# Attention and a routed MoE on one Trainium2 core: loads of q, k, v held to three in flight, and the stores of x moved

## The chip, the cores and the metric

The kernel runs on one core of one Trainium2 chip. The metric is the device time of one execution in microseconds (us). The core has a matrix engine (TensorE, "PE" in the profile; "PEld" is its weight load, which overlaps it), a vector engine (VectorE, "DVE"), a scalar engine (ScalarE, "ACT"), GpSimd ("POOL") and SyncE ("SP"), which here does nothing but issue DMAs and wait for them. Sixteen DMA engines move data between HBM and the on-chip memory. Matmul results land in PSUM, everything else on the chip is in SBUF.

## The reference, cut to what matters

```python
# q, k, v: (8 batches, 8 heads, 576 rows, 64), f32
kv  = einsum('bhsd,bhse->bhde', k, v)            # one 64x64 state for a head
out = einsum('bhsd,bhde->bhse', q, kv)
x   = out / sqrt(mean(out**2, -1) + 1e-6) * g_norm
x   = x.transpose(0, 2, 1, 3).reshape(4608, 512)  # N rows, D = 512
# MoE with early exit: E = 8 experts, F = 1024
do  = (x @ w_skip) > 0
e   = argmax(x[do] @ w_gate, 1);  gate = its softmax weight
y   = gate * (relu(x[do] @ w1[e]) @ w2[e])        # each row by its one expert
out = x;  out[do] = x[do] + y
```

## The kernel before, in words

**Order.** The whole program is written out by hand in one manual schedule: what stands first in the code is issued first on its engine. Two planning tables matter. `at(step, part, job)` puts a job at a place of a step, and a loop over `NU = 36` steps calls the places in the order `early`, `values`, `mid`, `norm`, `pe`, `end`. `portions` says in which steps the state of which batch is summed.

**Attention.** A step works on a unit: half of the heads of 256 rows of one batch. Two units make a pair (`nq`), and there are 18 pairs: two for each batch, and after every four batches one pair of the ninth rows that are left over. In a step PE turns q of the next unit (`turn`, L460, copied to SBUF by ACT as `qT`), multiplies q with the state and with the folded gate columns in one go (`values`, L498, and L508 for the left-over pairs), and sums a portion of k-times-v for the next batch (`state`, L383, eight matmul records for each group of 64 rows). ACT squares (L514) and takes roots (L529), DVE sums squares (L522) and scales (`xl`, L545), POOL multiplies by g (`xb`, L615). When all 18 groups of a batch are summed, ACT copies the state to `both` (L390), POOL and DVE each copy it twice into the block matrix `kvd` (L395 and L394), PE turns it (L400) and multiplies it with the gate weights (`state_m`, L408), and ACT copies those results into `kvd` (L412). All of these small products share one PSUM tile, `g_ps`.

**Loads.** SP issues every load of q, k, v (96 of them, 288 KB each) and most stores of x (`out_dram<-xb`, 256 KB each) in one order. Buffers: three of k and v, two of q, six of xb. A load of k and v is issued when the batch three before it has been summed. The framework gives DMAs eight semaphores in turn, so that a DMA waits for the one eight before it. A pair's x is stored in two halves when POOL has made it; of some pairs POOL issues the first half itself (L649).

**Gating.** Three groups of row tiles (`ends = [12, 22, 36]`) are gated while attention runs: `choose` on DVE, `rank` (running counts, matmuls into `g_ps`, L696 to L702), `number` on DVE (`oha_k`, L728). After the second group the experts are sorted by their counts (`rank_experts`, whose result `order_i` SP reads before it loads the first expert's w1, L337), and the first 192 rows of expert 0 are found among the batches 0 to 4 (`early`: 22 small matmuls L926, a sum on DVE L930, a small matmul L936) and gathered by POOL (L919). Batches 0 to 4 are the pairs 0 to 10. That gather waits for the stores of those pairs.

**Experts.** From about 117 us on the eight experts run one after the other (lines from L1157 on), nearly all of it PE. Their weights stand in two sets of buffers, `wpool_a` and `wpool_b`. The tile w2 of `wpool_a` is called `room` during attention, because until the first expert's w2 is loaded (L347) it only holds some small inputs. The gathers of later rows (L1148) wait for all stores of x.

Of the kernel before, what the change touches and what calls it, by code (L numbers as in the profile page):

```python
# [17 lines left out]
def kernel(  # L18
# [47 lines left out]
    P = 128  # L66
# [3 lines left out]
    NF = B // 4  # L70
    FQ = 4 * NQ + 1
    NT = NF * FQ * 2
    E, F = moe_w1.shape[0], moe_w1.shape[2]
    G = E + 1
    KD = D + G
# [34 lines left out]
    g_ps = ps_g.tile([P, 512], FP32)  # L110
    GB = 4 * KD + 8 * G

    kts, vts, qts = {}, {}, {}

    def load_part(t, src, b, j):

        js = slice(j, j + 1)
        nc.sync.dma_start(
            out=t[:, js, :, :].rearrange("p j c d -> p j (c d)"),
            in_=src[b].rearrange("(j a) (p c) d -> (a p) j (c d)", a=2, c=C)[:, js, :])  # L120

    def load(pool, tag, src, b):
        t = pool.tile([P, 4, C, D], FP32, tag=tag, name=tag)
# [120 lines left out]
    nc.vector.tensor_copy(out=eorder[:, :], in_=eorder_i[:, :])  # L244
    ebase = keep.tile([P, E], FP32)
    nc.vector.tensor_copy(out=ebase[:, :], in_=ebase_i[:, :])
    exp_f = keep.tile([P, E], FP32)
    nc.vector.tensor_copy(out=exp_f[:, :], in_=exp_i[:, :])
    col_f = keep.tile([P, CK], FP32)
# [101 lines left out]
            tc.add_manual_dep(ins.ins, behind.ins.name, WAIT, reason="gathers first")  # L351


    kvTs, boths = {}, {}

    def own(b, w):

# [17 lines left out]
    def state(b, some):  # L375

        kt, vt = kts[b], vts[b]
        for i in some:
            u, c = divmod(i, C)
            for w in range(2):  # L380
                for a in range(2):
                    r = slice(a * 64, (a + 1) * 64)
                    nc.tensor.matmul(  # L383
                        out=sum_ps[w * 64:(w + 1) * 64, a, u, :],
                        lhsT=kt[r, 2 * u + w, c, :], rhs=vt[r, 2 * u + w, c, :],
                        start=(c == 0), stop=(c == C - 1), skip_group_check=True)
        if some.stop < 2 * C:
            return
        both = att_pool.tile([P, 2, 2 * D], FP32, tag="both", name="both", bufs=1)
        nc.scalar.copy(out=both[:, :, :].rearrange("p u (a d) -> p a u d", a=2), in_=sum_ps)  # L390
        boths[b] = both
        cols = slice(G, G + 2 * D)
        for w in range(2):
            nc.vector.tensor_copy(out=other(b, w)[:, :, cols], in_=both[w * 64:(w + 1) * 64, :, :])  # L394
            nc.gpsimd.tensor_copy(out=own(b, w)[:, :, cols], in_=both[w * 64:(w + 1) * 64, :, :])  # L395

    def state_t(b):
        both = boths.pop(b)
# [38 lines left out]

    late = []
    todo = {}
    WAIT = mybir.DependencyInfo(mybir.DependencyClass.Sync, mybir.DependencyReason.SCHED_ONLY)  # L440

    def at(step, part, job):
        todo.setdefault((step, part), []).append(job)
# [323 lines left out]
    order_i = keep.tile([1, E], I32)  # L767
    is_at = keep.tile([P, E, E], FP32)

    def count_tokens(name, pool):  # L770
# [3 lines left out]

    def rank_experts():

        key = count_tokens("key", gat_pool)
        nc.vector.scalar_tensor_tensor(out=key[:, :], in0=key[:, :], scalar=float(E),
                                       in1=eorder[:, :], op0=ALU.mult, op1=ALU.add)
# [16 lines left out]
        order_f = gat_pool.tile([P, E], FP32, tag="order_f", name="order_f")  # L796
        yield
        nc.vector.tensor_reduce(out=order_f[:, :], in_=gt[:, :, :], axis=AX.X, op=ALU.add)
        yield
        nc.vector.tensor_copy(out=order_i[:, :], in_=order_f[0:1, :])  # L800
        yield
        nc.vector.scalar_tensor_tensor(
            out=colid_i[:, :].rearrange("p (r c) -> p r c", c=CK),
            in0=order_f[:, :].unsqueeze(2).to_broadcast([P, E, CK]), scalar=float(RSPACE // 128),
            in1=col_f[:, :].unsqueeze(1).to_broadcast([P, E, CK]), op0=ALU.mult, op1=ALU.add)
# [92 lines left out]
    def early():  # L898
# [24 lines left out]
        def put():  # L923
            scale(now[0])
            for t in range(NE):
                nc.tensor.matmul(out=ps, lhsT=oha_k[:, t, :],  # L926
                                 rhs=bv[:, t, :, :].rearrange("p c i -> p (c i)"), start=(t == 0),
                                 stop=(t == NE - 1), skip_group_check=True)
            rows = gat_pool.tile([P, 2], FP32, tag="rows1", name="rows1")
            nc.vector.tensor_reduce(out=rows[:, :], in_=ps.rearrange("p (c i) -> p c i", i=2),  # L930
                                    axis=AX.X, op=ALU.add)
            gather(rows[:, 0:1], P, 0)

            def put_more():
                more = g_ps[:, GB + 4:GB + 5]
                nc.tensor.matmul(out=more, lhsT=again[0, 64][:, :], rhs=rows[:, 1:2], start=True,  # L936
                                 stop=True, skip_group_check=True)
# [28 lines left out]
    for b, n in starts.items():  # L966
        if b:
# [6 lines left out]
                step += 1  # L974
            assert i == 2 * C and step < n and step - len(counts) > over - 1
            at(step, "early", lambda b=b: state_t(b))
            at(step, "pe", lambda b=b: state_m(b))
            over = step
        at(over, "end", lambda b=b: load_kv(b + 3, range(4 if b > 1 else 2)))
# [5 lines left out]
    def gating(g):  # L985

        yield from choose(g)
        yield lambda: rank(g)
        numbers = number(g)
        yield next(numbers)  # L990
        if g == LAST - 1:
# [3 lines left out]
        if g == LAST - 1:  # L995
            yield from early()

    streams = []
    now = [0]
    at(NU - 4, "pe", lambda: load_second(0, valued[-1]))  # L1000
    for r in range(1, E):
# [10 lines left out]
    PACE = (2, 4)  # L1012
    for n in range(NU + 2):
        now[0] = n
        if 1 <= n < NU - 1:
            turn(n + 1)
        if 1 <= n <= NU:
            root(n - 1)
# [3 lines left out]
        jobs(n, "mid")  # L1022
        if THIRD + 2 <= n < NU:
            squares(n)
        done = norm(n - 1) if 1 <= n <= NU else None
        if n < THIRD + 2:
            squares(n)
# [604 lines left out]
```

## Time and profile before

| what | value |
|---|---|
| median of three runs | 369.45 us (369.28 to 370.48) |
| the profiled execution | 369.93 us, of which the span of instructions is 368.1 us |
| PE busy | 349.5 us, 95% of the span |
| DVE, ACT, POOL busy | 249.2, 144.7, 126.6 us |
| DMA | 81.70 MB, mean 222 GB/s |
| granted TensorE clock | 1.00 |

The page divides the span into 40 slices of 9.2 us and gives each engine's busy share of a slice in tenths. "Idle before, releaser" is the time in which an engine stood still before an instruction, and what ended it; "issue" there means that the profile shows nothing that the engine waited for. Instructions are themselves fetched by DMA: those transfers are the queues of the kind "instruction".

### The profile page before, as it was taken

The page shows a single profiled execution, that of the slowest core. Times are in us where ns is not written, and L with a number is a line of the kernel's source. Part 1 is how long each engine was busy: PE and PEld are TensorE (multiplying, and loading weights), DVE is VectorE, ACT ScalarE, POOL GpSimd, SP SyncE. Part 2 cuts the span into 40 slices and gives each one's busy share as a digit, 9 for nine tenths or more (in the row PEclk, how much of TensorE's full clock was granted, in tenths as well). Part 3 has the DMA queues.
Part 4 walks back from the last instruction along what each step waited for, and adds up shares of the span by engine and source line. Part 5 has one row for each costly group of instructions (what it writes and reads, how often), then busy time and mean ns, then how long its engine had stood idle before and what let it go on. Part 6 is the DMA issues. An engine that isn't in the chain of part 4 may idle for free.

```text
span 368.1 us, 9568 instructions
## 1 busy us (share of the span) xinstructions
PE 349.5 (95%) x3754; PEld 304.4 (83%) x3754; DVE 249.2 (68%) x637; ACT 144.7 (39%) x418; POOL 126.6 (34%) x205
## 2 busy tenths in 40 slices
PE   8979997899889998999999999999999999999994
PEld 4768886788779668599879988988998988989983
DVE  2636677689889661776938675776776876878831
ACT  2537675466666242434204501421431430431420
POOL 8037777667776072223031203303203202002003
PEclk9999999999999999999999999999999999999999
DMA  8999999999977459972617345564663672601001
GB/s 274 383 389 387 393 389 396 401 357 328 325 247 268 116 183 367 363 250 78 230 54 251 98 198 184 176 232 123 223 231 80 241 249 56 244 1 49 11 1 54
DMA packets 32808, 81.70 MB, mean 222 GB/s; under 512 B 3242, under 2 KB 3250, under 8 KB 32756
## 3 DMA queue, kind: packets, MB, share of 16 engines
q1 hardware_dynamic: 28944, 69.48, 53.3%
q0 software_dynamic: 3792, 11.53, 9.3%
q8 instruction: 31, 0.51, 0.5%
q14 instruction: 21, 0.17, 0.1%
q10 hardware_dynamic: 20, 0.02, 0.0%
HBM read 66.80 MB, written 14.48 MB: 221 GB/s over the span
## 4 chain that ended last, share of the span: by engine, by line
PE 78%; issue 8%; DMA 5%; DVE 4%; POOL 3%; ACT 2%; SPq 0%; POOLq 0%; DVEq 0%; ACTq 0%
PE bank L1256 45%; PE bank L1188 8%; PE o_ps L498 6%; DMA v<-in_v_dram 4%; PE sum_ps L383 4%; PE bank L1176 3%; PE q_ps L460 3%; PE bank L1157 2%; DVE xl L545 1%; POOL xb L615 1%; PE g_ps L861 1%; DMA xg<-out_dram,asrc 1%; PE o_ps L508 1%; PE q_ps L861 1%; PE g_ps L762 1%
## 5 line engine op out<-in xcount | busy, mean ns | idle before, releaser
L1266 ACT COPY p<-bank 128x128 f32<-128x128 f32 (+6 forms) x70 | 20.8, 297 | 95.7 <-PE bank L1256 94.1
L1256 PE MATMUL bank<-xt,w 128*128 128x128 f32 (+5 forms) x336 | 55.5, 288 | 0.0
L1387 POOL DMA_INDIRECT out_dram<-xg,rows x14 | 14.0, 997 | 113.4 <-DVE xg L1384 111.1
L1256 PEld LDWEIGHTS bank<-xt,w 128*128 128x128 f32 x336 | 47.0, 190 | 1.9 <-DVE bank L1260 1.4
L615 POOL TENSOR_TENSOR xb<-xl,g_b 128x512 f32<-128x512 f32 x34 | 41.4, 1217 | 19.1 <-DVE rs L536 17.3
L1260 DVE TENSOR_TENSOR bank<-bank,p 128x128 f32<-128x128 f32 (+6 forms) x70 | 23.6, 337 | 29.1 <-PE bank L1256 27.7
L1256 PE MATMUL bank<-xs,s 128*128 128x128 f32 (+5 forms) x224 | 36.7, 288 | 0.0
L498 PE MATMUL o_ps<-kvd,qT 128*128 128x146 f32 x240 | 35.2, 288 | 1.3 <-DVE xl L545 1.0
L498 PEld LDWEIGHTS o_ps<-kvd,qT 128*128 128x128 f32 x240 | 31.4, 189 | 2.1 <-DVE xl L545 1.8
L1256 PEld LDWEIGHTS bank<-xs,s 128*128 128x128 f32 x224 | 31.1, 190 | 1.0 <-issue 0.5
L1188 PE MATMUL bank<-w,ht 128*32 128x128 f32 (+2 forms) x424 | 29.9, 313 | 0.0
L383 PE MATMUL sum_ps<-v,k 64*64 64x64 f32 x1152 | 24.4, 223 | 5.5 <-issue 4.6
L383 PEld LDWEIGHTS sum_ps<-v,k 64*64 64x64 f32 x1152 | 20.0, 134 | 10.0 <-issue 6.9
L545 DVE TENSOR_TENSOR xl<-o_ps,rs 128x584 f32<-128x584 f32 x32 | 24.5, 767 | 4.3 <-PE o_ps L498 0.5
L1188 PEld LDWEIGHTS bank<-w,ht 128*32 128x32 f32 (+2 forms) x424 | 18.2, 119 | 10.6 <-issue 7.2
L1256 PE MATMUL bank<-t,ht 128*128 128x256 f32 x112 | 27.0, 384 | 0.0
L522 DVE TENSOR_REDUCE rs<-sq 128x8 f32<-128x512 f32 x36 | 24.5, 680 | 3.7 <-ACT sq L514 3.6
L1256 PE MATMUL bank<-w,ht 128*128 128x256 f32 x112 | 26.5, 380 | 0.0
L1148 POOL DMA_INDIRECT xg<-out_dram,src x14 | 14.0, 998 | 36.3 <-DMA out_dram<-xg,rows 13.2
L1256 PE MATMUL bank<-t,hs 128*128 128x256 f32 x112 | 25.3, 379 | 0.0
L514 ACT ACTIVATE sq<-o_ps 128x512 f32<-128x512 f32 x34 | 20.3, 597 | 12.5 <-PE o_ps L498 11.8
L463 ACT COPY qT<-q_ps 128x512 f32<-128x512 f32 x32 | 18.8, 586 | 13.5 <-PE q_ps L460 13.3
(216 smaller groups left out, 667.5 us busy)
## 6 DMA issues: line engine op xcount, KB each, us to landing
w<-in_moe_w_dram SPq DMA_DIRECT2D x16, 2048.0 KB, 8.9
k<-in_k_dram SPq DMA_DIRECT2D x32, 288.0 KB, 6.0
v<-in_v_dram SPq DMA_DIRECT2D x32, 288.0 KB, 6.1
q<-in_q_dram SPq DMA_DIRECT2D x32, 288.0 KB, 5.8
out_dram<-xb SPq DMA_DIRECT2D x29, 256.0 KB, 6.4
out_dram<-xb POOLq DMA_DIRECT2D x7, 256.0 KB
xg<-out_dram,src POOLq DMA_INDIRECT x16
out_dram<-xg,rows POOLq DMA_INDIRECT x16
```

The costliest lines, as they stand in the source:

```text
L383: nc.tensor.matmul(out=sum_ps[w * 64:(w + 1) * 64, a, u, :], lhsT=kt[r, 2 * u + w, c, :], rhs=vt[r, 2 * u + w, c, :], start=(c == 0), stop ...
L463: nc.scalar.copy(out=qT[:, :, :, :].rearrange("p w a t -> p (w a t)"), in_=ps[:, :, :, :, :].rearrange("p w a h t -> p (w a h t)"))
L498: mm = nc.tensor.matmul(out=ps[:, w, 0:2 * PK].rearrange("p (r k) -> p r k", r=2)[:, :, cols], lhsT=qT[:, w, a, :], rhs=kvds[b % KVD][:, w ...
L514: nc.scalar.activation(out=sq[:, :, :, :], in_=heads(ps, G, G + 2 * D), func=ACT.Square)
L522: nc.vector.tensor_reduce(out=rs[:, :, :], in_=sq[:, :, :, :].rearrange("p x y (a d) -> p x (y a) d", a=2), axis=AX.X, op=ALU.add)
L545: nc.vector.tensor_tensor(out=xl[:, :, :, :].rearrange("p x y (a k) -> p x (y a) k", a=2), in0=ps[:, :, 0:2 * PK].rearrange("p x (h k) -> ...
L615: late.append((lambda eng: eng.tensor_tensor(out=xb[:, :, 4 * u * D:(4 * u + 4) * D].rearrange("p r (w x) -> p r w x", w=2), in0=xl[:, :, ...
L1148: nc.gpsimd.indirect_dma_start(out=x_of(xg, off, m), out_offset=None, in_=cut_rows(m)[:, :], in_offset=bass.IndirectOffsetOnAxis(ap=idx[:, ...
L1188: nc.tensor.matmul(out=yps[q * m:(q + 1) * m, 0:n], lhsT=ht(f)[:, off:off + m], rhs=w_sb[r][1][:, f, q * n:(q + 1) * n], start=(f == 0), s ...
L1256: nc.tensor.matmul(out=out, lhsT=lhsT(i), rhs=rhs(i), start=start and i == 0, stop=i == k - 1, skip_group_check=True)
L1260: nc.vector.tensor_tensor(out=to, in0=x, in1=y, op=ALU.add)
L1266: nc.scalar.copy(out=t, in_=x)
```

## The change

1. Each load of q, k, v from the thirteenth on also waits until the load three before it has landed (`PACED`, `DEPTH`). Stores are not counted.
2. x of the pairs 2 to 5 is written into `room` instead of an xb buffer, and is stored from the steps 20 to 23 on, behind the loads of q of batch 6. For these and all other pairs in `store_from` both halves are issued by SP, none by POOL.
3. x of the pairs 11 and later is stored from step `NU - 4` on, which is behind the load of the first expert's w2 and behind the first gathers.
4. `rank` moves from the place `pe` to `mid`, ahead of `state_m`.
5. The two copies of a state on DVE go to ACT for the batches 5 to 7 (`state_across`).
6. Sorting the experts takes three DVE instructions less (`kbase` is made beforehand, `order_i` is summed directly as integers).
7. In `early` q of the next unit is turned on PE between the 22 matmuls and the small one, and the rows are summed at the new place `squared`, behind the sum of squares of that step. Since fewer instructions stand ahead of it, DVE makes `bv`, on which the 22 matmuls work, ahead of the step's `xl`; before, it came behind the sum of squares that follows `xl`.

```diff
-        nc.sync.dma_start(
+        ins = nc.sync.dma_start(
...
+        if len(loads) >= PACED:
+            tc.add_manual_dep(ins.ins, loads[-DEPTH].ins.name, WAIT, reason="a short queue")
+        loads.append(ins)
...
         for w in range(2):
-            nc.vector.tensor_copy(out=other(b, w)[:, :, cols], in_=both[w * 64:(w + 1) * 64, :, :])
+            if b < ACROSS:
+                nc.vector.tensor_copy(out=other(b, w)[:, :, cols], in_=both[w * 64:(w + 1) * 64, :, :])
             nc.gpsimd.tensor_copy(out=own(b, w)[:, :, cols], in_=both[w * 64:(w + 1) * 64, :, :])
+    def state_across(b, w):
+        if b >= ACROSS:
+            nc.scalar.copy(out=other(b, w)[:, :, G:G + 2 * D], in_=boths[b][w * 64:(w + 1) * 64, :, :])
...
-            xbs[nq] = xb_pool.tile([P, 2, DM], FP32, tag="xb", name="xb")
+            if nq in IN_ROOM:
+                x = room[:, IN_ROOM.index(nq) * 2 * DM:(IN_ROOM.index(nq) + 1) * 2 * DM]
+                xbs[nq] = x.rearrange("p (r d) -> p r d", r=2)
+            else:
+                xbs[nq] = xb_pool.tile([P, 2, DM], FP32, tag="xb", name="xb")
...
-    store_from = {x[0]: starts[B - 3] + 2 for x in units if x[1:3] in ((0, None), (4, 0))}
+    IN_ROOM = range(2, 6)
+    store_from = {nq: starts[B - 3] - 2 + i for i, nq in enumerate(IN_ROOM)}
+    store_from.update({nq: starts[B - 3] + 2 for nq in (4 * NQ, 4 * NQ + 1)})
+    store_from.update({nq: NU - 4 for nq in range(KNOWN_PAIRS, NT // 2)})
...
-        first = int(i == 1 and b < B - 1)
+        first = int(i == 1 and b < B - 1 and nq not in store_from)
...
-            rows = gat_pool.tile([P, 2], FP32, tag="rows1", name="rows1")
...
+            turn(now[0] + 2)
+            turned_ahead.append(now[0] + 2)
+            def put_rows():
+                rows = gat_pool.tile([P, 2], FP32, tag="rows1", name="rows1")
...
-            at(now[0], "pe", put_more)
+            at(now[0], "squared", put_rows)
...
-        yield lambda: rank(g)
+        yield "mid", lambda: rank(g)
```

On SP, from the loads of q of the last batches to the first expert's weights, this stood before (`w_1851` and `w_1853` are w1 and w2 of the first expert, `order_i` the sorted experts):

```order
L653 DMA out_dram<-xb 64x1024 x3
L118 DMA q<-in_q_dram 128x576 x8
L642 DMA out_dram<-xb 64x2x512 x2
L653 DMA out_dram<-xb 64x1024 x3
L816 TENSOR_LOAD order_i
L337 ISA
L337 DMA w_1851<-in_moe_w_dram 128x4x1024
L653 DMA out_dram<-xb 64x1024 x5
L347 ISA
L347 DMA w_1853<-in_moe_w_dram 128x8x512
L653 DMA out_dram<-xb 64x1024 x3
```

And this stands there now (`w_115` is `room`, with x of the pairs 2 to 5):

```order
L674 DMA out_dram<-xb 64x1024 x3
L121 DMA q<-in_q_dram 128x576 x4
L674 DMA out_dram<-w_115 64x1024 x8
L121 DMA q<-in_q_dram 128x576 x4
L663 DMA out_dram<-xb 64x2x512 x2
L674 DMA out_dram<-xb 64x1024 x3
L835 TENSOR_LOAD order_i
L346 ISA
L346 DMA w_1846<-in_moe_w_dram 128x4x1024
L356 ISA
L356 DMA w_1848<-in_moe_w_dram 128x8x512
L674 DMA out_dram<-xb 64x1024 x10
```

Eight stores moved between the last two batches' loads of q, and no store stands between the two weight loads any more.

On PE, at the left-over rows of the first four batches, the product of the state with the gate weights stood ahead of the first group's counts before:

```order
L508 MATMUL o_ps<-kvd_170,q_403 64x73
L408 MATMUL g_ps<-gw_b,kvT 128x36 x2
L696 MATMUL g_ps<-top,ident 128x104
L699 LDWEIGHTS ut
L699 MATMUL g_ps<-ohb,ut 128x96
```

Now it stands behind them, the counts' last matmul first in these rows:

```order
L723 LDWEIGHTS ones
L723 MATMUL g_ps<-ohb,ones 128x8
L422 MATMUL g_ps<-gw_b,kvT 128x36 x2
L473 MATMUL q_ps<-ident,q 128x2x64 x4
```

`state_m` changed places with `rank`; the same happens at the second group.

On PE, at the first gather, the small matmul that moves the last 64 rows (`again`) followed at once on the matmuls that find them (`oha_k`):

```order
L926 MATMUL g_ps<-bv_1981,oha_k 128x4
L936 MATMUL g_ps<-rows_2023,again_64_243 128x1
L460 MATMUL q_ps<-ident,q 128x2x64 x4
L479 MATMUL o_ps<-ident,q 128x128 x2
```

Now the turn of q stands between them:

```order
L945 MATMUL g_ps<-bv_1948,oha_k 128x4
L473 MATMUL q_ps<-ident,q 128x2x64 x4
L957 MATMUL g_ps<-rows_2023,again_64_245 128x1
L492 MATMUL o_ps<-ident,q 128x128 x2
```

PE has work there while DVE sums the rows that the small matmul needs.

More of the change, by code (lines that the diff above doesn't have):

```diff
@@ L72 @@
     NT = NF * FQ * 2
+    KNOWN_PAIRS = 11
     E, F = moe_w1.shape[0], moe_w1.shape[2]
@@ L111 @@
     GB = 4 * KD + 8 * G
-    kts, vts, qts = {}, {}, {}
+    kts, vts, qts, loads = {}, {}, {}, []
+    PACED, DEPTH = 12, 3
+    WAIT = mybir.DependencyInfo(mybir.DependencyClass.Sync, mybir.DependencyReason.SCHED_ONLY)
     def load_part(t, src, b, j):
         js = slice(j, j + 1)
-        nc.sync.dma_start(
+        ins = nc.sync.dma_start(
             out=t[:, js, :, :].rearrange("p j c d -> p j (c d)"),
             in_=src[b].rearrange("(j a) (p c) d -> (a p) j (c d)", a=2, c=C)[:, js, :])
+        if len(loads) >= PACED:
+            tc.add_manual_dep(ins.ins, loads[-DEPTH].ins.name, WAIT, reason="a short queue")
+        loads.append(ins)
     def load(pool, tag, src, b):
@@ L246 @@
     nc.vector.tensor_copy(out=ebase[:, :], in_=ebase_i[:, :])
+    kbase = keep.tile([P, E], FP32)
+    nc.vector.scalar_tensor_tensor(out=kbase[:, :], in0=ebase[:, :], scalar=-float(E),
+                                   in1=eorder[:, :], op0=ALU.mult, op1=ALU.add)
     exp_f = keep.tile([P, E], FP32)
@@ L351, in load_second @@
             tc.add_manual_dep(ins.ins, behind.ins.name, WAIT, reason="gathers first")
-    kvTs, boths = {}, {}
+    kvTs, boths, ACROSS = {}, {}, 5
     def own(b, w):
@@ L393, in state @@
         for w in range(2):
-            nc.vector.tensor_copy(out=other(b, w)[:, :, cols], in_=both[w * 64:(w + 1) * 64, :, :])
+            if b < ACROSS:
+                nc.vector.tensor_copy(out=other(b, w)[:, :, cols], in_=both[w * 64:(w + 1) * 64, :, :])
             nc.gpsimd.tensor_copy(out=own(b, w)[:, :, cols], in_=both[w * 64:(w + 1) * 64, :, :])
+    def state_across(b, w):
+        if b >= ACROSS:
+            nc.scalar.copy(out=other(b, w)[:, :, G:G + 2 * D], in_=boths[b][w * 64:(w + 1) * 64, :, :])
     def state_t(b):
-        both = boths.pop(b)
+        both = boths[b]
         for u in range(2):
@@ L439 @@
     todo = {}
-    WAIT = mybir.DependencyInfo(mybir.DependencyClass.Sync, mybir.DependencyReason.SCHED_ONLY)
     def at(step, part, job):
@@ L766 @@
     colid_i = keep.tile([P, NCOL], I32)
-    order_i = keep.tile([1, E], I32)
+    order_i = keep.tile([P, E], I32)
     is_at = keep.tile([P, E, E], FP32)
@@ L775, in rank_experts @@
     def rank_experts():
-        key = count_tokens("key", gat_pool)
-        nc.vector.scalar_tensor_tensor(out=key[:, :], in0=key[:, :], scalar=float(E),
-                                       in1=eorder[:, :], op0=ALU.mult, op1=ALU.add)
+        key = gat_pool.tile([P, E], FP32, tag="key", name="key")
+        nc.vector.scalar_tensor_tensor(out=key[:, :], in0=top[:, :], scalar=float(E),
+                                       in1=kbase[:, :], op0=ALU.mult, op1=ALU.add)
         gt = gat_pool.tile([P, E, E], FP32, tag="gt", name="gt")
@@ L795, in rank_experts @@
                                 in1=exp_f[:, :].unsqueeze(1).to_broadcast([P, E, E]), op=ALU.mult)
-        order_f = gat_pool.tile([P, E], FP32, tag="order_f", name="order_f")
         yield
-        nc.vector.tensor_reduce(out=order_f[:, :], in_=gt[:, :, :], axis=AX.X, op=ALU.add)
-        yield
-        nc.vector.tensor_copy(out=order_i[:, :], in_=order_f[0:1, :])
+        with nc.allow_low_precision(reason="whole numbers"):
+            nc.vector.tensor_reduce(out=order_i[:, :], in_=gt[:, :, :], axis=AX.X, op=ALU.add)
         yield
@@ L803, in rank_experts @@
             out=colid_i[:, :].rearrange("p (r c) -> p r c", c=CK),
-            in0=order_f[:, :].unsqueeze(2).to_broadcast([P, E, CK]), scalar=float(RSPACE // 128),
+            in0=order_i[:, :].unsqueeze(2).to_broadcast([P, E, CK]), scalar=float(RSPACE // 128),
             in1=col_f[:, :].unsqueeze(1).to_broadcast([P, E, CK]), op0=ALU.mult, op1=ALU.add)
@@ L928, in put @@
                                  stop=(t == NE - 1), skip_group_check=True)
-            rows = gat_pool.tile([P, 2], FP32, tag="rows1", name="rows1")
[L930 to L934, printed above, removed]
+            turn(now[0] + 2)
+            turned_ahead.append(now[0] + 2)
+            def put_rows():
+                rows = gat_pool.tile([P, 2], FP32, tag="rows1", name="rows1")
+                nc.vector.tensor_reduce(out=rows[:, :], in_=ps.rearrange("p (c i) -> p c i", i=2),
+                                        axis=AX.X, op=ALU.add)
+                gather(rows[:, 0:1], P, 0)
                 more = g_ps[:, GB + 4:GB + 5]
@@ L938, in put_more @@
                 gather(more, 64, P)
-            at(now[0], "pe", put_more)
+            assert now[0] == THIRD + 2
+            at(now[0], "squared", put_rows)
+        yield
+        yield
         yield "mid", put
@@ L976 @@
             at(step, "early", lambda b=b: state_t(b))
+            for w, part in enumerate(("early", "mid")):
+                at(step, part, lambda b=b, w=w: state_across(b, w))
             at(step, "pe", lambda b=b: state_m(b))
@@ L996, in gating @@
             yield from early()
-    streams = []
+    streams, turned_ahead = [], []
     now = [0]
@@ L1014 @@
         now[0] = n
-        if 1 <= n < NU - 1:
+        if 1 <= n < NU - 1 and n + 1 not in turned_ahead:
             turn(n + 1)
@@ L1024 @@
             squares(n)
+        jobs(n, "squared")
         done = norm(n - 1) if 1 <= n <= NU else None
```

## The prediction

> **What bounds the kernel now.** I read the slices first, then the idle time of PE, then what stands on the DMA queues where PE idles. First the page's slices (40 of 9.2 us) and the stretches of 5 us that matter:
>
> ```profile
> PE   8979997899889998999999999999999999999994
> DMA  8999999999977459972617345564663672601001
> 5.00:10.00 5.00, 4.96 (x92) 2.95 (x91) 1.27 (x18) 0.72 (x3) 3.20 (x6) 1.00 1.01 367
> 20.00:25.00 5.00, 2.58 (x83) 2.22 (x81) 1.56 (x3) 1.38 (x3) 1.19 (x1) 1.00 1.05 389
> 60.00:65.00 5.00, 2.75 (x66) 2.33 (x66) 3.16 (x9) 2.65 (x8) 2.91 (x5) 1.00 1.05 399
> 95.00:100.00 5.00, 3.97 (x33) 3.73 (x34) 4.78 (x15) 3.56 (x11) 3.77 (x8) 1.00 0.98 319
> 115.00:120.00 5.00, 5.00 (x63) 4.93 (x63) 4.77 (x13) 3.34 (x14) 2.26 (x2) 1.00 0.49 192
> ```
>
> The columns of the stretches are PE, PEld, DVE, ACT and POOL busy, then clock, DMA share and GB/s. PE is full except in places of attention, and DMA is full for the first 90 us. From 110 us on PE is full again, so what attention saves before that arrives at the end, and nothing else can be saved by this change. The idle places are in the timeline of PE:
>
> ```profile
> 18.33 1.26 PE L383 MATMUL sum_ps<-v,k 64*64 64x64 f32 x68 [0.77 <-DMA v<-in_v_dram]
> 24.45 0.62 PE L383 MATMUL sum_ps<-v,k 64*64 64x64 f32 x25 [2.42 <-issue]
> 35.38 0.66 PE L460 MATMUL q_ps<-ident,q 128*128 128x128 f32 x4
> 45.85 0.66 PE L460 MATMUL q_ps<-ident,q 128*128 128x128 f32 x4
> 61.49 0.47 PE L696 MATMUL g_ps<-top,ident 128*128 128x104 f32 x2 [0.96 <-ACT kvd L412]
> 65.13 0.57 PE L383 MATMUL sum_ps<-v,k 64*64 64x64 f32 x21 [1.42 <-issue]
> 71.52 0.56 PE L383 MATMUL sum_ps<-v,k 64*64 64x64 f32 x18 [0.74 <-issue]
> 86.05 0.46 PE L696 MATMUL g_ps<-top,ident 128*128 128x88 f32 x2 [0.44 <-ACT kvd L412]
> 98.24 1.26 PE L498 MATMUL o_ps<-kvd,qT 128*128 128x146 f32 x8 [1.03 <-DVE xl L545]
> 101.80 0.69 PE L926 MATMUL g_ps<-bv,oha_k 128*128 128x4 bf16 x22 [0.65 <-DVE bv L906]
> 102.74 0.38 PE L936 MATMUL g_ps<-rows,again 128*128 128x1 f32 x2 [0.25 <-DVE rows L930]
> ```
>
> Three waits (2.42, 1.42, 0.74 us) end on "issue" in the middle of a run of equal matmuls, and a wait for a load would name it, as the one at 18.33 does. In the stretch of each there is one packet of an instruction queue among the loads; here 21.5 to 24.5 us (packets, MB, share of 16 engines), and ahead of it two lines of the whole page:
>
> ```profile
> PE 349.5 (95%) x3754; PEld 304.4 (83%) x3754; DVE 249.2 (68%) x637; ACT 144.7 (39%) x418; POOL 126.6 (34%) x205
> q8 instruction: 31, 0.51, 0.5%
> ...
> q1 hardware_dynamic: 558, 1.14, 102.9%
> q8 instruction: 1, 0.02, 2.2%
> ```
>
> The page counts 31 such packets, 0.51 MB, so 16 KB each, for 7508 matmul and weight records, so one packet is some 240 instructions, and the sums of k and v, with 68 matmuls and as many weights in 1.26 us, use one up in some 2.3 us. I read these three waits as PE out of instructions, the fetch being late behind loads. How deep the loads stand shows the timeline of SP and the median of landings:
>
> ```profile
> 18.76 0.33 SPq L118 DMA_DIRECT2D k<-in_k_dram  x1
> 19.51 0.33 SPq L118 DMA_DIRECT2D v<-in_v_dram  x1
> 20.26 0.33 SPq L118 DMA_DIRECT2D k<-in_k_dram  x1
> k<-in_k_dram SPq DMA_DIRECT2D x32, 288.0 KB, 6.0
> ```
>
> One load every 0.75 us, landing after 6.0 us: eight in flight, the engines saturated.
>
> **The change part by part.** All terms are against the profiled execution (span 368.1, time 369.93 us) and are carried over to the median of 369.45, which is 0.48 us lower.
>
> *Period of a load.* With three in flight a load cannot come faster than the 0.75 us of the rows above. The other end is a queue that runs empty between loads:
>
> ```profile
> DMA  0000000000000995966798599308796995900000
> out_dram<-xb SPq DMA_DIRECT2D x2, 256.0 KB, 3.0
> ```
>
> This is 118.8 to 122.5 us in 40 slices of 0.0925 us: two stores into an idle queue, first data 13 slices after the start, landing after 3.0 us. With 288 KB instead of 256 that is 3.1 us, over three 1.03 us a load. I take 0.80: the stretch from 5 to 10 us, when the queue was still filling, moved 367 GB/s, and 288 KB at that rate take 0.80 us. It is the nearest row, since two other loads (1.5 us of transfer) stand ahead while a third starts up for about 1.2 us. [...]
>
> *What the loads permit.* In SP's order the 16th load is the one that PE waits for at 18.33, the 38th is the second of q of batch 2 (needed at 35.38), the 50th that of batch 3 (needed at 45.85), with two stores of x between. That 16th load took 8 us because eight loads shared the engines:
>
> ```profile
> 9.97 8.02 DMA v<-in_v_dram
> ```
>
> With fewer ahead and none behind I put it at 17.0 instead of 18.0. Then the 38th lands at 17.0 + 22 x 0.80 = 34.6 and the 50th at 17.0 + 34 x 0.80 + 1.3 (two stores of 0.65) = 45.5. So of the waits before that, 0.77 and 2.42, which both go, only 0.35 us (45.85 less 45.5) is kept; q is late next. Behind this the loads gain on PE again, since k and v of a batch are not asked for before a buffer is free.
>
> *Fetches.* The waits at 65.13 and 71.52 go: -1.42 - 0.74 = -2.16. A fetch then stands behind at most three loads. If nothing changes for it, this is 0; more than the whole wait it cannot be.
>
> *Counts ahead of the gate product.* PE waited 0.96 and 0.44 us for ACT's copies out of `g_ps`. With `rank` first, PE needs only the older copy kvT. -1.40. What is queued behind the counts, L408 and ACT's L412 copies, comes about 1 us later; the matmul that reads them comes some steps later.
>
> *First gather.* `bv` made ahead removes the 0.65 us, but delays `xl` by its own 0.24, which is in the same DVE chain and hidden unless PE waits there; the 0.25 us at L936 is covered by the turn of q. I book -0.65 and leave the 0.25 for the delay of `xl`.
>
> *State copies to ACT.* DVE is full at 95 to 100 us (4.78 of 5):
>
> ```profile
> 95.08 0.69 DVE L394 COPY kvd<-both 64x256 f32<-64x256 f32 x2
> 96.12 1.06 DVE L728 TENSOR_TENSOR oha_k<-row_i,lo_i 128x256 bf16<-128x256 int32 x2
> 90.46 0.16 DVE L800 CAST order_i<-order_f 1x8 int32<-1x8 f32 x1
> 94.23 0.35 ACT L482 COPY q<-o_ps 64x256 f32<-64x256 f32 x1
> ```
>
> There 0.69 goes and a third `oha_k` of 0.53 moves in: -0.16 on the wait of 1.03. ACT takes six copies; the nearest row is the last, 0.35 us each, and ACT is at 3.56 of 5. The first of each pair stands ahead of Square: hidden for the batches 5 and 6 where DVE has room, +0.35 once for batch 7 (0 to 1.05 as bounds). The three DVE instructions less in sorting are like the third row, 0.16 us each, beside PE's work: 0.
>
> *Stores.* Moved out of the loads' time: 0 by itself, it is in the period of the loads. Eight stores ahead of the last q cost 5.2 us on the queue, in a stretch where q of batch 7 is needed only at 96.57 us (row below). Of the POOL DMAs four go: 0, POOL is not waited for. After the first expert's w2 (issued at 106.40) now stand 14 stores: 2.1 + 3.7 MB at the 389 GB/s of the stretch from 20 us end at about 121 us, and the gather that needs them is at 129.13:
>
> ```profile
> 96.57 0.64 PE L460 MATMUL q_ps<-ident,q 128*128 128x128 f32 x4
> 106.40 0.39 SPq L347 DMA_DIRECT2D w<-in_moe_w_dram  x1
> 129.13 1.06 POOL L1148 DMA_INDIRECT xg<-out_dram,asrc  x1 [10.16 <-DVE arows L1131]
> ```
>
> It is released by DVE. If that cover went, the stores would cost what they end after 129.
>
> Sum: -0.35 - 2.16 - 1.40 - 0.65 - 0.16 + 0.35 = -4.37, so 369.45 becomes **365.1 us** (the profiled execution 365.6).
>
> **The rivals.** *A, too short a queue, slower.* If three in flight give 1.03 us a load, the 50th load lands at 17.0 + 34 x 1.03 + 1.3 = 53.3, 7.5 us late, at the turn of q for batches 2 and 3. The later terms give 4.0 back: +3.5, 373.0 us. It decides from 0.93 us a load on, where 34 x 0.93 + 18.3 is 4.0 over 45.85. For it: 3.0 us into an idle queue. Against: with two loads ahead the queue is not idle. [...]
>
> *B, the fetch does not wait behind loads.* Then the waits on "issue" stay, loads or not, and -2.16 and -0.35 drop out: 369.45 - 1.86 = 367.6. For it: fetches go by a queue of their own, q8. Against: from 110 us on, with the DMA share at half (0.49 in 115 to 120), PE runs without such waits; but its instructions are longer there. [...]
>
> *C, PE gains and hands back.* PE comes earlier to 93 to 106 us, where DVE is full, and waits there for `xl`: the gain of 4.4 shrinks to what DVE gave up, about 0.2 + 0.65: 368.6, or nothing with ACT's copies exposed (1.05), 369.5. Against: DVE's chain starts from PE's products, so it comes earlier too.
>
> **How the numbers follow.** Chances: the forecast (362.5 to 366.8) 0.47; more than that, with every wait gone, below 362.5, 0.06; the middle of A (about 368) 0.09; A itself, above 370.6, 0.18; B 0.11; C 0.09. Within 0.3% (1.1 us, about what a measurement of this kernel can tell from no change, 368.3 to 370.6) come half of the middle of A and most of C: 0.12. Slower is A, 0.18; faster the rest, 0.70. The range leaves out the 0.06 below and the worse part of A: **362.5 to 372.0**; the forecast's own is 362.5 to 366.8.
>
> **What the profile would show.** Right: landings of k, v, q near 2.4 us, SP issuing one in 0.80 us, no wait on "issue" over 0.5 us at the sums of k and v, no wait of L696's successor for L412, PE idle in attention 4 to 5 us shorter. Wrong: PE waiting at the turns of q (L460's successor) for DMA q near 34, 46 or 87 us, DMA share below 0.8 in the first 90 us, landings at 2.8 us or more; or the waits on "issue" at the same size behind a shorter queue; or the first gather late, and PE waiting for xg near 105.

## The result, and the profile after

The changed kernel takes 406.75 us (median; 403.79 to 410.21) where the kernel before has 369.62 us: a ratio of 1.098 [1.095, 1.102]. The forecast was 365.1 us. The profiled execution has a span of 405.0 us, 36.9 us more than before. These are the page's lines of it: busy times, slices of PE, the clock and DMA (now 10.1 us each), and the shares of the chain that ended last:

```profile
PE 365.0 (90%) x3754; PEld 317.9 (78%) x3754; DVE 247.5 (61%) x630; ACT 147.6 (36%) x424; POOL 123.5 (30%) x201
...
PE   8876689796778689989999999999999999999994
...
PEclk9988798988969979999999999999999999999999
DMA  8878888788977994499734455266365455610101
...
PE 62%; DMA 28%; issue 5%; SPq 2%; ACT 1%; POOL 1%; DVE 1%; POOLq 0%; ACTq 0%; DVEq 0%
```

PE's idle time went from 368.1 - 349.5 = 18.6 us to 405.0 - 365.0 = 40.0 us, and the same 3754 matmul records take 15.5 us longer, because the granted clock fell in places (its mean is 0.95 instead of 1.00). DMA is at 7 to 8 tenths in the first 90 us, where it was full, and 28% of the last chain is DMA. The longest waits of PE (total, times, longest), and the places in its timeline:

```profile
PE q_ps L473 <- DMA q<-in_q_dram: 18.1, 12, 5.3
PE sum_ps L392 <- DMA v<-in_v_dram: 6.9, 6, 2.3
PE q_ps L869 <- DMA xg<-out_dram,src: 4.5, 1, 4.5
```

```profile
23.99 1.69 PE L392 MATMUL sum_ps<-v,k 64*64 64x64 f32 x68 [2.33 <-DMA v<-in_v_dram]
44.65 0.41 PE L473 MATMUL q_ps<-ident,q 128*128 128x128 f32 x2 [2.15 <-DMA q<-in_q_dram]
61.45 0.41 PE L473 MATMUL q_ps<-ident,q 128*128 128x128 f32 x2 [2.38 <-DMA q<-in_q_dram]
77.34 0.47 PE L717 MATMUL g_ps<-top,ident 128*128 128x104 f32 x2
80.66 0.44 PE L473 MATMUL q_ps<-ident,q 128*128 128x128 f32 x2 [1.99 <-DMA q<-in_q_dram]
95.38 0.41 PE L473 MATMUL q_ps<-ident,q 128*128 128x128 f32 x2 [2.50 <-DMA q<-in_q_dram]
114.24 1.34 PE L473 MATMUL q_ps<-ident,q 128*128 128x128 f32 x4 [5.28 <-DMA q<-in_q_dram]
130.06 0.44 PE L473 MATMUL q_ps<-ident,q 128*128 128x128 f32 x2 [0.40 <-DMA q<-in_q_dram]
133.19 0.38 PE L957 MATMUL g_ps<-rows,again 128*128 128x1 f32 x2 [0.45 <-DVE rows L953]
143.07 1.09 PE L869 MATMUL q_ps<-ident,xg 128*128 128x128 f32 x4 [4.53 <-DMA xg<-out_dram,src]
```

PE now waits for q at the turns of every batch from batch 2 on (the batches are numbered from 0). The profile shows no wait on issue at the sums any more, and the counts (L717) have no wait in front of them. But the small matmul of the first gather, at 102.74 us before, is at 133.19 us: 30.45 us later. From there to the end lie 271.8 us instead of 265.4, and the 4.53 us for the first gather and some 2.2 us of a low clock behind it account for that difference (a clock of 0.77 from 143 to 153 us, row below).

Why the loads are late shows the chain in order of time (start, us, what). It hangs on one landing after the other:

```profile
12.47 4.27 DMA v<-in_v_dram
16.76 3.35 DMA k<-in_k_dram
20.13 3.73 DMA v<-in_v_dram
23.87 4.84 DMA q<-in_q_dram
...
53.72 3.28 DMA k<-in_k_dram
57.02 5.05 DMA q<-in_q_dram
...
127.27 2.74 DMA q<-in_q_dram
136.25 6.69 DMA xg<-out_dram,src
```

Each row is a load that the third load behind it waited for, so from the row of 12.47 (the 14th load) to that of 57.02 (the 50th) lie twelve landings and 36 loads: 44.55 us, or 3.71 us a landing and **1.24 us a load**. The 50th lands at 62.07 us. The last load, issued at about 84.3 us before, is issued at 127.27. The rate is in the stretches (columns as in the prediction), with two places of low clock, and the landing in the table of DMA issues (count, size, median us):

```profile
18.00:58.00 40.00, 30.43 (x515) 27.16 (x516) 15.14 (x31) 15.71 (x42) 15.73 (x30) 0.83 0.82 251
115.00:120.00 5.00, 5.00 (x49) 4.52 (x50) 2.41 (x7) 1.81 (x4) 1.40 (x2) 0.50 0.86 271
143.00:153.00 10.00, 9.93 (x110) 9.19 (x111) 4.96 (x18) 5.49 (x20) 3.25 (x7) 0.77 1.03 394
```

```profile
k<-in_k_dram SPq DMA_DIRECT2D x32, 288.0 KB, 3.6
```

The same stretch of the kernel before moved 389 GB/s:

```profile
18.00:58.00 40.00, 36.82 (x766) 32.67 (x766) 25.76 (x54) 24.98 (x66) 26.58 (x51) 1.00 1.04 389
```

### The profile page after: what moved, and what is told of

Read it like the earlier page. It is cut to its first block, busy times and chain, and to the rows that moved or that the text cites. A ratio compares the mean times of both kernels' runs of the same rounds, so it can differ in the third digit from the quotient of the medians.

```text
span 405.0 us, 9564 instructions
## 1 busy us (share of the span) xinstructions
PE 365.0 (90%) x3754; PEld 317.9 (78%) x3754; DVE 247.5 (61%) x630; ACT 147.6 (36%) x424; POOL 123.5 (30%) x201
## 4 chain that ended last, share of the span: by engine, by line
PE 62%; DMA 28%; issue 5%; SPq 2%; ACT 1%; POOL 1%; DVE 1%; POOLq 0%; ACTq 0%; DVEq 0%
PE bank L1283 41%; DMA q<-in_q_dram 10%; DMA k<-in_k_dram 9%; PE bank L1215 9%; DMA v<-in_v_dram 7%; PE bank L1203 4%; PE bank L1184 2%; PE o_ps L511 2%; DMA xg<-out_dram,src 2%; SPq L674 1%; PE q_ps L473 1%; PE g_ps L880 1%; PE q_ps L880 1%; PE g_ps L783 1%; POOL out_dram L1437 0%
## 5 line engine op out<-in xcount | busy, mean ns | idle before, releaser
L632 POOL TENSOR_TENSOR xb<-xl,g_b 128x512 f32<-128x512 f32 x26 | 31.7, 1218 | 40.2 <-DVE rs L549 34.8
L473 PE MATMUL q_ps<-ident,q 128*128 128x128 f32 x128 | 25.6, 317 | 18.2 <-DMA q<-in_q_dram 18.1
L511 PE MATMUL o_ps<-kvd,qT 128*128 128x146 f32 x240 | 41.6, 323 | 0.3
L511 PEld LDWEIGHTS o_ps<-kvd,qT 128*128 128x128 f32 x240 | 37.9, 222 | 1.1 <-DVE xl L558 0.6
L473 PEld LDWEIGHTS q_ps<-ident,q 128*128 128x128 f32 x128 | 15.1, 156 | 22.9 <-issue 12.7
L392 PE MATMUL sum_ps<-v,k 64*64 64x64 f32 x1152 | 26.5, 234 | 6.9 <-DMA v<-in_v_dram 6.9
L392 PEld LDWEIGHTS sum_ps<-v,k 64*64 64x64 f32 x1152 | 22.1, 145 | 11.8 <-issue 6.9
L549 DVE RECIPROCAL rs<-rs 128x8 f32<-128x8 f32 x36 | 7.2, 199 | 37.3 <-ACT rs L542 37.3
L558 DVE TENSOR_TENSOR xl<-o_ps,rs 128x584 f32<-128x584 f32 x32 | 24.5, 767 | 3.9
## 6 DMA issues: line engine op xcount, KB each, us to landing
w<-in_moe_w_dram SPq DMA_DIRECT2D x16, 2048.0 KB, 10.1
```

What stands on the lines that cost most here:

```text
L392: nc.tensor.matmul(out=sum_ps[w * 64:(w + 1) * 64, a, u, :], lhsT=kt[r, 2 * u + w, c, :], rhs=vt[r, 2 * u + w, c, :], start=(c == 0), stop ...
L473: nc.tensor.transpose(out=ps[:, w, :, hf, :], in_=qts[b][:, 2 * u + w, c:c + 2, :], identity=ident[:, :])
L511: mm = nc.tensor.matmul(out=ps[:, w, 0:2 * PK].rearrange("p (r k) -> p r k", r=2)[:, :, cols], lhsT=qT[:, w, a, :], rhs=kvds[b % KVD][:, w ...
L558: nc.vector.tensor_tensor(out=xl[:, :, :, :].rearrange("p x y (a k) -> p x (y a) k", a=2), in0=ps[:, :, 0:2 * PK].rearrange("p x (h k) -> ...
L632: late.append((lambda eng: eng.tensor_tensor(out=xb[:, :, 4 * u * D:(4 * u + 4) * D].rearrange("p r (w x) -> p r w x", w=2), in0=xl[:, :, ...
```

## The experiments

The theory after this result: three loads in flight do not keep the DMA engines busy, a load then takes 1.24 us, and everything in attention waits for that. The rivals: the moved stores or other parts of the change do it; or the low clock is half of the loss; or the rate of a held queue is low whatever its size. Besides, the terms that the forecast had booked as gains were to be seen alone. Each ratio is against the kernel before on the same chip.

**One part undone, one part alone, other depths.** Four kernels: no load held (`PACED = 1000`); four in flight; six in flight; and the kernel before with nothing but the holding to three.

```diff
 # e1_no_pace            # e2_depth4 / e3_depth6
-    PACED, DEPTH = 12, 3      -    PACED, DEPTH = 12, 3
+    PACED, DEPTH = 1000, 3    +    PACED, DEPTH = 12, 4   (12, 6)
 # e4_before_depth3: the kernel before, load_part alone changed
+    PACED, DEPTH = 12, 3
...
+        if len(loads) >= PACED:
+            tc.add_manual_dep(ins.ins, loads[-DEPTH].ins.name, PACE_WAIT, reason="a short queue")
+        loads.append(ins)
```

> The changed kernel with no load held back; the eight semaphores alone bound the queue, as before. Theory 1 (the whole loss is the short queue: three in flight bring a load every 1.1 to 1.2 us instead of 0.75, PE waits for q and v, and its clock drops after the waits): 363 to 368 us, clock 1.00, PE waits for q and v under 2 us in all. Theory 2 (the stores put between the loads of q and behind the first weights cost a good part, since the largest waits, 5.28 us for q of batch 6 and 4.53 us for the first gather, stand there): over 373 us, with those two waits still there. A short queue's own gain, the waits on issue of 2.42, 1.42 and 0.74 us, should be lost again here by both.

> Four loads in flight instead of three. Theory 1: a load still lands in about 3.5 us, so one comes every 0.9 us, PE waits little, the clock drops in few places or none: 368 to 380 us. Theory 2: above 390 us, since the stores stand where they stood.

> Six in flight. Theory 1: the engines are saturated, 0.75 us a load, landing 4.5 us: 363 to 367 us. If instruction fetches wait behind loads, the waits on issue at the sums of k and v are smaller than with eight in flight (sum under 3 us against 4.6). Theory 2: above 373 us.

> The kernel before with nothing but the loads held to three in flight, stores where they were. Theory 1: 400 to 412 us, as the whole change or a little worse, since the stores of pairs 2 to 5 and 11 and later still stand among the loads. Theory 2: under 390 us.

| kernel | us | ratio |
|---|---|---|
| change without holding | 369.46 | 0.999 [0.996, 1.003] |
| six in flight | 375.45 | 1.013 [1.007, 1.019] |
| four in flight | 388.88 | 1.051 [1.046, 1.055] |
| three, on the kernel before | 405.53 | 1.098 [1.091, 1.104] |

The kernel before has 369.88 us on this chip. Holding to three, alone, costs all of it, and without it the rest of the change is worth nothing. The moved stores are not the cause. Only the last of the four lies in its first range. The run without holding lies just above its own (363 to 368), four in flight between its two ranges (368 to 380, above 390), and six in flight misses 363 to 367: at six, the deepest of them, the loads do not keep their rate either. The stretch from 18 to 58 us and the landing of k, first with four and then with six in flight:

```profile
18.00:58.00 40.00, 30.46 (x563) 27.32 (x555) 18.01 (x35) 17.51 (x47) 18.47 (x36) 0.86 0.88 284
```

```profile
k<-in_k_dram SPq DMA_DIRECT2D x32, 288.0 KB, 4.2
```

```profile
18.00:58.00 40.00, 33.78 (x670) 29.54 (x670) 22.15 (x46) 22.77 (x61) 22.41 (x43) 1.00 0.98 338
```

```profile
k<-in_k_dram SPq DMA_DIRECT2D x32, 288.0 KB, 5.1
```

With 3, 4, 6 and 8 in flight the rate is 251, 284, 338 and 389 GB/s, and the landing 3.6, 4.2, 5.1 and 6.0 us; landing over depth gives 1.20, 1.05, 0.85 and 0.75 us a load. A shorter queue shortened the landing, but less than in proportion.

**The clock.** bf16 products that nobody uses are given to PE ahead of the first turn of q of the batches 2 to 6, so that it does not stand idle there.

```diff
+    FILL = {2: 12, 3: 9, 4: 7, 5: 9, 6: 19}
     def turn(n):
         ...
+        if i == 0 and u == 0 and b in FILL:
+            dense(FILL[b], ps[:, :, :, :, :].rearrange("p w a h t -> p (w a h t)"))
```

> The kernel after, with PE given bf16 products of 128x512 into the tile that the turn of q then overwrites (12, 9, 7, 9 and 19 of them, 0.27 us each) ahead of the first turn of q of the batches 2 to 6, where PE waits for q in the profile after. Their results are used by nobody. Theory 'the loads set the time': in attention PE is never waited for by the loads (the SP queue waits for PE 0.8 us in all there), so the matmuls of the stretch that run at a clock of 0.5 to 0.9 run inside time that the loads take anyway. The clock then rises to 0.98 or more, PE busy holds the 15 us of new products, and the time falls only by what the low clock costs after the last load (143 to 153 us at 0.77, 2.3 us): 402 to 407 us. Rival 'half the loss is the clock': PE's 15.5 us of longer busy time are on the path, and the time falls to about 391 us.

402.15 us, ratio 1.092 [1.082, 1.101], which overlaps that of the change itself. The page's line of busy times; the stretch up to PE's wait for the first gather, in the change (to 138.54 us) and here (to 137.70 us); and that wait here:

```profile
PE 371.0 (93%) x3810; PEld 316.9 (79%) x3810; DVE 248.0 (62%) x630; ACT 147.6 (37%) x424; POOL 124.8 (31%) x201
```

```profile
0.00:138.54 138.54, 110.62 (x1766) 93.41 (x1766) 72.35 (x201) 65.94 (x173) 66.12 (x133) 0.89 0.82 258
0.00:137.70 137.70, 117.30 (x1822) 92.89 (x1822) 72.22 (x201) 65.97 (x173) 67.94 (x137) 0.95 0.86 265
```

```profile
PE q_ps L873 <- DMA xg<-out_dram,src: 1.9, 1, 1.9
```

In the trace the 56 new products take 12.95 us (about 0.23 us each, less than the 0.27 expected). So the old ones take 371.0 - 12.95 = 358.1 us instead of 365.0: 6.9 us of the 15.5 are won back. Of these, 6.3 lie ahead of the wait for the gather (110.62 against 117.30 - 12.95 = 104.35), and yet PE comes to that wait only 0.84 us earlier. Of the 4.8 us by which the span fell, 0.84 are these, 2.6 are the shorter wait itself and 1.3 lie behind it. So the low clock inside attention was mostly hidden behind the loads, as the first theory says, and 391 us is out by far. The test is partial: the other 8.6 us of low clock were not removed, and the two profiles are from different chips, on which the kernel before differs by 1.0 us.

**Count or bytes.** Three in flight, each load from batch 1 on twice the size.

```diff
-    def load_part(t, src, b, j):
-        js = slice(j, j + 1)
+    def load_part(t, src, b, j, w):      # w = 2 if b else 1, j in steps of w
+        js = slice(j, j + w)
```

> The kernel after, with the loads of k, v and q from batch 1 on made of two of the old ones each (576 KB instead of 288 KB), three at a time as before. Theory 'a fixed time per load': a load's landing has a part that does not grow with its bytes, and three of 288 KB do not cover it; with the double size it is paid half as often, the bytes in flight are those of six old loads, and the time is near that of six in flight, 373 to 379 us. Rival 'the wait itself is what costs' (SP's issue, the semaphore and the count of three, whatever the size): per byte it is halved too, but the loads then come late for the first turns that need half of one, 385 to 395 us. Rival 'rate': the engines give a single queue with three transfers only 260 GB/s, whatever their size: 404 to 408 us.

380.27 us, ratio 1.032 [1.025, 1.039], just above the first theory's range and below the second's. The stretch, the landing, and the longest wait of PE:

```profile
18.00:58.00 40.00, 31.41 (x581) 28.69 (x574) 18.31 (x37) 18.20 (x49) 18.63 (x37) 0.87 0.91 296
```

```profile
k<-in_k_dram SPq DMA_DIRECT2D x14, 576.0 KB, 6.0
```

```profile
42.58 1.09 PE L475 MATMUL q_ps<-ident,q 128*128 128x128 f32 x4 [4.62 <-DMA q<-in_q_dram]
```

The rate rises from 251 to 296 GB/s, so it is not a fixed property of a held queue. Twice the bytes land in 6.0 instead of 3.6 us; on a straight line through these two medians 1.2 us of a landing do not grow with the bytes (0.4 to 1.7 with the medians of q and v). It stays below the 338 GB/s of six single loads with the same bytes, so the bytes in flight are not all of it. How much the number in flight and the coarser steps each make is not settled.

**Where a short queue helps.** Do the waits on issue belong to the depth of the load queue? Only the loads 65 to 82 are held, to four.

```diff
-        if len(loads) >= PACED:
+        if len(loads) in PACED:
...
-    PACED, DEPTH = 12, 3
+    PACED, DEPTH = range(64, 82), 4
```

> The kernel after, with only the loads 65 to 82 held, to four in flight; all others are free as before. These are in flight when PE waits on issue at 65.0 and 71.5 us in the run without pacing (1.45 and 0.84 us). Theory 'the fetch of instructions waits behind the loads': both waits go below 0.4 us, the last load is issued some 3 to 4 us later and just in time, and the time is 366.5 to 368 us. Rival 'the fetch does not wait behind loads': the waits stay at 1.4 and 0.8 us, 369 to 371 us. If the loads are too late for the q of batch 6 or 7, PE waits there and the time is 370 to 373 us with the issue waits gone.

372.74 us, ratio 1.010 [1.006, 1.014]. The waits on issue at the sums in the run without holding, then the first wait of more than 0.7 us behind 60 us here, and the rate from 60 to 65 us:

```profile
24.08 0.69 PE L392 MATMUL sum_ps<-v,k 64*64 64x64 f32 x25 [1.88 <-issue]
...
64.98 0.57 PE L392 MATMUL sum_ps<-v,k 64*64 64x64 f32 x21 [1.45 <-issue]
71.46 0.56 PE L392 MATMUL sum_ps<-v,k 64*64 64x64 f32 x19 [0.84 <-issue]
```

```profile
73.28 0.41 PE L473 MATMUL q_ps<-ident,q 128*128 128x128 f32 x2 [1.55 <-DMA q<-in_q_dram]
```

```profile
60.00:65.00 5.00, 4.35 (x100) 3.84 (x98) 3.74 (x11) 3.32 (x10) 3.46 (x6) 1.00 0.82 282
```

Both waits on issue are gone, before PE waits for q (in their stretch it waits only 0.65 us, for `xl`), so they do belong to the depth of the load queue. Waits for q stand in their place (4.2 us in all), and the kernel is slower. It is the third of the expected cases.

That these waits are late fetches can be counted in the traces. Take PE's instructions (weight loads, matmuls and semaphore instructions) in order of start. In the kernel before, the waits of 2.42, 1.42 and 0.74 us stand behind 705, 2241 and 2497 of them: 6 x 256 and 256 apart. Every such wait at the sums, in the kernel before and in all the experiments, stands at one of these counts, or at one further whole multiples of 256 away. And those three ended 1.48, 1.49 and 1.39 us after the end of a 16 KB packet of the instruction queue. I read this as PE out of instructions, with 256 of them in a packet, close to the 240 that the prediction estimated. At the wait of 1.42 us the packet started to move when PE had 2155 instructions behind it, 86 short of the 2241.

**A milder hold, and the rest alone.** Six in flight for the loads 65 to 82; the same for the loads 21 to 34 as well; and the kernel before with the counts, `bv` and sorting items of the change, without and with that window.

```diff
 # f1_window6: the change, and
+    PACED, DEPTH = range(64, 82), 6
 # f2_two_windows6: the change, and
+    PACED, DEPTH = [*range(20, 34), *range(64, 82)], 6
 # e8_counts_bv: items 4, 6 and 7 of the change on the kernel before
+    PACED, DEPTH = 1000, 3
 # f3_counts_window6: the same, and
+    PACED, DEPTH = range(64, 82), 6
```

> The kernel before, with the counts ahead of the gate product, bv made ahead of the first gather and the three instructions less in sorting, and nothing else of the change: loads free, x stored as before, the state copies on DVE. By the prediction's terms -1.40 and -0.65 the time is 367 to 368.3 us where the kernel before has 369.5 to 369.9. Rival 'PE gains and hands back at DVE': 369 to 370 us, with a longer wait for xl near 97 us. If it is well below the run of the change without pacing (369.46), then the moved stores or ACT's copies cost what these gain.

> The kernel after, with only the loads 65 to 82 held, now to six in flight instead of four; all others free. The step from four to six takes 18 x 0.1 us = 2 us off the last load. Theory 'the fetch waits behind the loads, and six are few enough': PE has no wait on issue over 0.5 us at the sums near 65 and 71 us, q comes 1 us late at most, 367 to 369 us. Rival 'what a short queue gives to the fetch it takes from the loads': the issue waits go and waits for q of the same 1.5 to 2.5 us stand in their place, 369 to 371 us. Rival 'the fetch needs four': the issue waits stay above 0.7 us, 369 to 370 us.

> The kernel after, with the loads 21 to 34 and 65 to 82 held to six in flight; all others free. The first stretch is in flight when PE waits on issue at 24.08 us (1.88 us without pacing). Theory 'the fetch waits behind the loads': that wait falls to about 1 us, as it did with all loads at six, the loads of q of batch 2 come 14 x 0.1 = 1.4 us later, and the time is 366 to 369 us. Rival 'given back at q': PE waits for q near 36 us for 0.8 us or more, 369 to 372 us.

> The kernel before, with the counts ahead of the gate product, bv ahead of the first gather and the three instructions less in sorting, and the loads 65 to 82 held to six in flight; x stored as before, state copies on DVE. If the moved stores make the room that a short queue needs, this is slower than the same window with the moved stores, by 1 to 2 us: 369 to 371 us, with the waits for q in the place of the waits on issue. If the room is not from the stores, the two are equal within 0.5 us.

| kernel | us | before | ratio |
|---|---|---|---|
| counts, bv, sorting alone | 368.61 | 368.62 | 1.001 [0.998, 1.004] |
| change, one window of six | 366.89 | 367.00 | 1.002 [0.999, 1.004] |
| change, two windows of six | 367.41 | 367.00 | 1.001 [0.999, 1.003] |
| counts etc., one window of six | 368.19 | 367.00 | 1.004 [1.002, 1.007] |

None beats the kernel before. (The ratios are not the quotients of the two medians shown.) The times in the last three expectations were taken from chips on which the kernel before needs 369 to 370 us; here it needs 367.00, so that 366.89, just below the first range, is no gain, nor is the 367.41 with two windows, which lies in its first range. With two windows the first wait on issue falls to 0.78 us, and q takes it back 13 us later:

```profile
22.53 0.62 PE L392 MATMUL sum_ps<-v,k 64*64 64x64 f32 x25 [0.78 <-issue]
...
35.98 0.41 PE L473 MATMUL q_ps<-ident,q 128*128 128x128 f32 x2 [1.94 <-DMA q<-in_q_dram]
```

With one window of six the wait near 65 us stays at 0.90 us on the change, and at 2.28 us on the other base:

```profile
64.32 0.57 PE L392 MATMUL sum_ps<-v,k 64*64 64x64 f32 x21 [0.90 <-issue]
```

```profile
64.42 0.57 PE L392 MATMUL sum_ps<-v,k 64*64 64x64 f32 x21 [2.28 <-issue]
```

So six in flight do not remove these waits for certain. With three loads of double size, the same bytes in flight, two of them were left too (0.63 and 1.32 us). Whether the moved stores make room is not settled: the means of these two kernels lie 1.4 us apart (plus or minus 1.1), but they differ in ACT's copies of the state as well. With the counts and `bv` alone, the waits that these items were to remove are gone, and others have grown:

```profile
83.21 0.20 PE L717 MATMUL g_ps<-ohb,ut 128*128 128x80 bf16 x1 [0.57 <-DVE ohb L703]
...
96.82 1.26 PE L511 MATMUL o_ps<-kvd,qT 128*128 128x146 f32 x8 [1.19 <-DVE xl L558]
101.78 0.38 PE L954 MATMUL g_ps<-rows,again 128*128 128x1 f32 x2 [1.02 <-DVE rows L950]
```

Of the 1.40 + 0.65 us, 0.57 + 0.16 + 0.77 us come back at DVE (1.19 was 1.03, and 1.02 was 0.25). The 0.55 us left is below what the measurement tells.

## Why the prediction was wrong, point by point

*Period of a load: the step that failed.* 0.80 us was taken and 1.24 us measured, outside even the upper end of 1.03. The argument was that two loads ahead carry the engines over the start of a third. They do not: the DMA share fell from 1.04 to 0.82, and the same share moved less, too (251 / 0.82 = 306 GB/s for a full share, 389 / 1.04 = 374 before). The 0.80 was taken from the stretch of 5 to 10 us, where up to eight loads are in flight: a queue that fills, and not a short one. The 3.0 us of two stores in an idle queue, the nearer row, was put aside, and it was too low as well: with three loads in flight a landing took 3.71 us.

*What the loads permit.* The 50th load was to land at 45.5 us and landed at 62.07. The sentence that failed beside it is that the loads gain on PE again afterwards. With 1.24 us they lose at every batch, as the waits for q up to 130 us show, and the last load is 43 us late where the queue had a few us in hand. So rival A was the right case, priced at 373.0 because it let the delay end after batch 3. Reckoned its way, even 1.24 us a load gives only 380 us (17.0 + 34 x 1.24 + 1.3 = 60.5, 14.6 us late, less 4.0); the rest of the loss is the delay of the later batches, the late first gather and the low clock behind it. The middle of A among the chances (about 368 us) stands on a period between 0.80 and 1.03 us that no run shows for three in flight: it was 1.24 us there, and landing over depth gave 1.05 and 0.85 us with four and six.

*Fetches.* Right in mechanism: the waits on issue go when fewer loads are in flight (none with three and four; 1.05 us once with all loads at six, but 0.90 and 2.28 us in windows of six) and stay with eight (1.88, 1.45 and 0.84 us). With three, PE waits for v or q ahead of the first two places, which gives the fetch time as well; the window of four is the cleaner proof. Rival B falls. But the term was booked as a net gain, while the short queue that brings it delays the loads by as much or more: the single windows show the exchange.

*Counts, first gather.* The waits of 0.96, 0.44 and 0.65 us went, as said. The claim that the turn of q covers the wait for `rows` failed: 0.25 us became 0.80 us without holding and 1.02 us with these items alone. The handing back at DVE was rival C, and for these terms it was right.

*State copies.* The wait of 1.03 us for `xl` near 97 us is 0.45 us in the run without holding, more than the 0.16 us booked; 0.52 us for `xl` at 110.56 us came in its place:

```profile
97.15 1.26 PE L511 MATMUL o_ps<-kvd,qT 128*128 128x146 f32 x8 [0.45 <-DVE xl L558]
102.11 0.38 PE L957 MATMUL g_ps<-rows,again 128*128 128x1 f32 x2 [0.80 <-DVE rows L953]
...
110.56 0.74 PE L521 MATMUL o_ps<-kvd,q 64*64 64x73 f32 x32 [0.52 <-DVE xl L558]
```

*Stores.* Nothing by themselves, as booked. Named among the signs of being wrong, but given no price, was the first gather behind late loads: in the kernel before the first expert's w1 (2 MB) was issued at 91.76 us, 11.7 us ahead of the gather, and now at 133.23, 3.0 us ahead of it. The gather took 6.69 us to land, and PE waited 4.53. With four in flight w1 was issued 7.1 us ahead, the gather landed after 3.4 us, and PE did not wait. The gather was also issued 3.06 us behind the small matmul, where it was 0.68 us before; what held it is not shown.

*The clock.* The prediction did not speak of it, since it was 1.00 throughout. It is real (15.5 us of PE); of the 6.3 us that the new products won back ahead of the gather, some 5.4 were not on the path.

## What to carry to other kernels

Before a queue of transfers is shortened, take its period from landings at that depth: here a landing shrank less than the depth did, and the saturated queue's period (0.75 us) said nothing about the short one's (1.24 us). A wait that a shorter queue removes is a gain only where the loads are needed later than they land; ask at each later use how many us they are ahead. And where the loads set the pace, a stall's second cost, a lower clock, can be mostly hidden behind the next stall, as it was here (some 5.4 of the 6.3 us won back).

## What the runs showed of the hardware

The granted clock fell after some waits and not after other, longer ones. Without holding, a wait of 1.88 us that ended at 24.08 us was followed by half the clock, from 24.5 to 27.9 us; in the kernel before, a wait of 2.42 us at the same place, which ended at 24.45 us, by none. The stretch behind it, without holding and before:

```profile
25.00:27.50 2.50, 2.50 (x13) 2.50 (x12) 1.38 (x4) 1.23 (x4) 1.97 (x6) 0.50 1.05 364
```

```profile
25.00:27.50 2.50, 2.50 (x25) 2.34 (x21) 1.12 (x4) 1.86 (x5) 1.67 (x6) 1.00 1.07 389
```

So 1.88 us without work on PE stood ahead of half the clock, and 2.42 us ahead of the full one; what decided between the two is not shown.

The loads issued by SP, three in flight, landed after 3.6 us (the median of k), with a period of 1.24 us.
